# A linear-attention block with a gated FFN in split float32: four x tiles turned on VectorE through DRAM, a carried product in the down projection, and a new instruction order

## Chip, core and metric

The kernel runs on one core of one Trainium2 chip. The metric is the device time of one execution in microseconds (us). Engines: TensorE (PE, matmuls; PEld is its weight load), VectorE (DVE), ScalarE (ACT), GpSimd (POOL), SyncE (SP, which here only issues DMAs).

## The reference

S = 2048 tokens, D = 512, 32 heads of 16, F = 1792, all float32:

```python
xn = layernorm(x)
q, k, v = split(xn @ wqkv)
phi = lambda t: where(t > 0, t + 1, exp(t)) + 1e-6
pq, pk = phi(q), phi(k)
kv = einsum("bhsd,bhse->bhde", pk, v);  z = einsum("bhsd->bhd", pk)
o = einsum("bhqd,bhde->bhqe", pq, kv) / (einsum("bhqd,bhd->bhq", pq, z)[..., None] + 1e-6)
s = o @ wo
g = silu((gelu(xn @ w_gate) * (xn @ w_up)) @ w_down)
return x + s * g
```

v is never made: the kernel sums pk^T xn over the tokens (the tiles gps), multiplies it by wv and wo once, and gets a 512x512 matrix M, so that s = (pq / den) @ M.

## The kernel before

**Numbers.** A float32 matmul takes several passes of TensorE. The kernel instead writes a value as hi + lo, both in the type fp32r (the helper `split`: a cast on ACT for hi, a subtraction on DVE or POOL for lo), and does three one-pass matmuls, hi hi, hi lo and lo hi (`three`, issued by `Sum.add`, L531).

**Products.** The large products use Strassen's method in Winograd's form: seven products of half-size blocks for eight. Product 1 is copied by ACT from one bank of PSUM (X) into another (Y) as a seed, so that two results share it. This holds for k and q (`rest`, `first_products`), for gate and up (`quad`: 28 quads of seven products) and for the down projection (`down_strassen`: two passes p = 1 and 0 of NU = 7 steps u, each in two halves r, with seven products of three matmuls). Products 2, 6, 5, 7, 3, 4 go on in the banks X, Y and Z; six results of each half are added by DVE to the sums `acc` in SBUF, or copied there by ACT where u = 0 and the sum is new.

**Stages.** Stage A (to about 140 us) takes the 16 tiles of 128 tokens in eight pairs (`tokens`, NP = 8): load x, normalise (`ln`: statistics and xn on DVE, the power on POOL), transpose by PE into PSUM (`transp`: four 128x128 transposes a tile, L696, an ACT copy behind), split, multiply; q goes to DRAM (`q_d`). Pairs 0 and 1 are done with plain products, the others with Strassen's. 14 matmuls on a constant (`warm`, L561; 28 instructions, 5.82 us in the timeline) stand ahead of the first transposition. Between the stages come z (`run_z`, two split matmuls), kv and M. Then the FFN runs for the second half of the tokens (p = 1) and for the first (p = 0). Some work for later stages is done beside it: `prep_early` splits the weights of three quads and stores them in DRAM, `den` makes the denominators of a tile, `turn` loads a tile of q, divides it, transposes it by VectorE's 32x32 squares and stores it in `t_d`. The host has permuted the columns of wq so that the squares suffice.

**The end.** `attn` loads a chunk of 512 tokens of the turned q, splits it, and multiplies by M: chunk 2 behind pass 1, chunk 3 among the last down products, then chunks 0 and 1 (CHUNKS). `out_tile` loads x^T (`sxr`), multiplies the product by g, adds x^T and stores; the very last tile in two halves of columns, behind one matmul sum.

**The order.** Nothing is issued in program order. `do` records each operation with an engine and a duration; `Plan.order` lays them out with a forward pass over the engines, from latest start times; `KEPT` is a list of random alterations of these start times (a stretch of time and a seed each) that are applied one after the other. PE's order is first stated by hand in `pe_keys` and may be altered within `AHEAD` = 6 us. `forward` holds a model of the DMA queue (`RATES`, `HELD`, `BEHIND`). The engines in `ENGINES` run in exactly this order; SP is not among them before. `plan.due` makes an operation urgent from a given time on.

Of the kernel before, what the change touches and what calls it, by code (L numbers as in the profile page):

```python
# [9 lines left out]
F32 = mybir.dt.float32  # L10
# [9 lines left out]
    (85, 100, [10000006]),  # L20
    (70, 85, [10000048]),
    (-1, 12, [10000061]),
    (40, 55, [10000175]),
    (135, 200, [10000200]),
    (25, 40, [10000230]),
    (40, 55, [10000342]),
    (85, 100, [10000376]),
    (40, 55, [10000415, 10000462]),
    (500, 560, [10000471]),
    (-1, 12, [10000515]),  # L30
    (500, 560, [10000523, 10000590, 10000640]),
    (115, 135, [10000649]),
    (500, 560, [10000723]),
    (115, 135, [10000785]),
    (500, 560, [10000819, 10000833]),
    (340, 420, [10000924]),
    (115, 135, [10000994]),
    (-1, 12, [10001161, 10001223, 10001300]),
    (270, 340, [10001313, 10001357]),
    (-1, 12, [10001377]),  # L40
    (500, 560, [10001410]),
    (-1, 12, [10001492]),
    (40, 55, [10001818]),
    (-1, 12, [10001854]),
    (500, 560, [10001973]),
    (340, 420, [10002732]),
    (135, 200, [10006848]),
    (85, 100, [10010611]),
    (270, 340, [10010753]),
    (40, 55, [10010839]),  # L50
    (340, 420, [10010858]),
    (500, 560, [10010942, 10011053]),
    (40, 55, [10011765]),
    (135, 200, [10011937]),
    (-1, 12, [1010000092]),
    (340, 420, [1010000637, 1010002072]),
    (25, 40, [1010003933]),
    (500, 560, [1010016325, 1010018040]),
    (70, 85, [1010018047, 1010018667, 1010018893, 1010020523]),
    (55, 70, [1010020607]),  # L60
    (85, 100, [1010021997]),
    (100, 115, [1010030646]),
    (115, 135, [1010032131]),
    (100, 115, [1010033698]),
    (500, 560, [1010034750, 1010034866]),
    (135, 200, [1010038225]),
# [5 lines left out]
RATES = 260.0, 385.0  # L72
HELD = 1.3, 2.6
# [3 lines left out]
WARM = 14, 3  # L77
ENGINES = {mybir.EngineType.PE, mybir.EngineType.Activation, mybir.EngineType.DVE, mybir.EngineType.Pool}
# [52 lines left out]
class Plan:  # L131
# [179 lines left out]
    def forward(self, pe):  # L311
# [9 lines left out]
        while any(cands.values()):  # L321
# [43 lines left out]
            if o.eng == "SP":  # L365

                if written > o.end:
                    o.end = free["SP"] = max(o.end, dma - BEHIND)
                dma = max(dma, o.end) + o.kb / (RATES[0] if o.end < 3.0 else RATES[1])
# [26 lines left out]
def kernel(  # L396
# [78 lines left out]
    q_d = dram_view([NT, KT, P, P], "q_d", NT)  # L475
    g_d = dram_view([D, S // 2], "g_d", NT // 2)
    t_d = dram_view([KT, P, S], "t_d", NT)
    s_d = dram_view([D, NC], "s_d", KT)
# [70 lines left out]
    ones = const("ones", [P, P])  # L549
# [3 lines left out]
    ident = const("ident", [P, P])  # L553
# [9 lines left out]
    idle = bank(0, "warm", (P, P))  # L563
    do("PE", 0.427 * 10, warm, idle, ones, key="warm")
# [59 lines left out]
    CL = 2  # L624
    a21 = [[tile_in("up", 15 + 2 * lo + k, [P, D], F32R, f"a21{lo}{k}") for k in range(2)] for lo in range(2)]
# [8 lines left out]
    def ln(*ts):  # L634
        n = len(ts)
        mv = little("mv", f"mv{ts[0]}", [P, n, 2])
        for i, t in enumerate(ts):
# [7 lines left out]
           rstd, ve, neg_half)  # L645
        for i, t in enumerate(ts):
            xns[t] = U("xn", range(4, 9), f"xn{t}")
            do("DVE", 0.46, lambda o, i, m, r: nc.vector.tensor_scalar(o, i, m, r, op0=ALU.subtract, op1=ALU.mult),
               xns[t], xs.pop(t), mv[:, i, 0:1], rstd[:, i:i + 1], name=f"xn{t}")
# [38 lines left out]

    def transp(n, i):
        t = tokens[n][i]  # L690

        pt = bank(3 + 2 * n + i if 0 < 2 * n + i < 2 * CL else 1, f"pt{t}", (P, KT, P))

        def run(o, a, b):
            for k in range(KT):
                nc.tensor.transpose(o[:, k, :], a[:, k * P:(k + 1) * P], b)  # L696
            if n == 0 and i == 0:
                warm(idle(), ones(), WARM[1])
        do("PE", 0.4, run, pt, xns[t], ident, key=("T", n, i), name="T", more=(idle,) if n == 0 and i == 0 else ())
# [3 lines left out]
        xts[n, i] = v.part((v.res[i],), (slice(None), i))  # L703
        copy("ACT", xts[n, i], pt, D, f"xt{n}{i}")
        pts[n, i] = pt
# [16 lines left out]
    def split_x(n, i):  # L722
        if i == 0 and n == 0:
            for s in range(2):
                split(xrows("h", s, s + 1, [0]), xrows("l", s, s + 1, [0]), pts[0, 0][:, 2 * s:2 * s + 2], 2 * P, "Xa")
# [13 lines left out]
    def split_xn(t):  # L739
        h = U("xnh", range(9, 12), f"xnh{t}", F32R)  # L740
        lo = U("xnl", range(12, 15), f"xnl{t}", F32R)
        copy("ACT", h, xns[t], D, "xnh")
        tt("DVE", "sub", lo, xns[t], h, D, "xnl")
# [97 lines left out]
    for n in range(NP):  # L841
        if n == 0:
            ln(tokens[n][1])
        else:
            ln(*tokens[n])
        for i in range(2):
            load_next()
            transp(n, i)
            split_x(n, i)
# [42 lines left out]
    pe_keys.append(("T", 0, 0))  # L892
# [64 lines left out]
    EARLY = range(11, 14)  # L957
# [5 lines left out]

    GT = []
# [6 lines left out]
    ones_r = const("ones_r", [P, P], F32R)  # L971
    copy("ACT", ones_r, ones, P)
    zh, zl = tile_in("up", 34, [P, D], F32R, "zh"), tile_in("up", 35, [P, D], F32R, "zl")
    split(zh, zl, zacc, D, "z")
    pz = bank(7, "pz")

    def run_z(o, a, h, lo):
        nc.tensor.matmul(o, a, h, start=True, stop=False)
# [25 lines left out]
    def den(p, t):  # L1004
# [5 lines left out]
        do("DVE", 0.11, lambda o, i: nc.vector.tensor_add(o, o, i), r.map(lambda ap: ap.rearrange("p (s h) -> p s h", s=KT)),  # L1010
           den_eps.map(lambda ap: ap.unsqueeze(1).to_broadcast([P, KT, H // KT])))
        do("DVE", 0.28, lambda o: nc.vector.reciprocal(o, o), r, port=False)

    mask2 = const("mask2", [P, P])
# [113 lines left out]
    def h_sums(p, u):  # L1128
        def t():
            i = ring("hsum", range(4))  # L1130
# [6 lines left out]

    def down_strassen(p, u, first):

        for r in range(2):  # L1140
# [6 lines left out]
            def out(ps, key, new=False):  # L1147

                half, chunk = {11: (0, 0), 21: (1, 0), 12: (0, 1), 22: (1, 1)}[key]
                o = acc[p, 4 * chunk + 2 * half + r]  # L1150
                if first and new:
# [276 lines left out]
```

## Time and profile before

| | |
|---|---|
| time, median of 3 runs | 604.92 us (604.47 to 605.88) |
| the profiled execution's own time | 605.64 us |
| its span, first to last instruction | 603.5 us |
| granted TensorE clock, mean | 0.997 |
| DMA packets and bytes | 73384, 137.09 MB, mean 227 GB/s |

The span is shorter than the execution's time by what lies ahead of the first and behind the last instruction. In tables of groups a row gives line, engine, operation, output<-inputs, shapes and count, then busy time, mean ns of one, idle time just before and what ended it. Matmuls overlap, so that the mean of one is longer than the distance from one to the next. In the rows of time the first number is the start in us, the second the length.

### The profile page before, as it was taken

Reading aid. Unit: us, or ns where it says so; the run is one execution under the profiler, and the core shown is the slowest. Engines: PE = TensorE matmul, PEld = TensorE weight load, DVE = VectorE, ACT = ScalarE, POOL = GpSimd, SP = SyncE. Lnnn points to the kernel's source line nnn. Section 1 sums busy time; section 2 is a strip of 40 time slices with the busy share of each in tenths; the row PEclk is TensorE's granted clock in tenths of the full one; section 3 lists DMA queues with packets and bytes.
Section 4 is the critical chain, followed back from the end, with each engine's and each line's share of the span. In section 5 each row is a group of like instructions: output and inputs, shape, how many; then the busy total and the mean of one; then the engine's idle time right before and its main releaser. Section 6 shows DMA issues by size and latency. Waiting matters only on the chain.

```text
span 603.5 us, 7883 instructions
## 1 busy us (share of the span) xinstructions
PE 594.2 (98%) x2636; PEld 483.4 (80%) x2636; DVE 517.0 (86%) x819; ACT 347.1 (58%) x627; POOL 243.0 (40%) x237
## 2 busy tenths in 40 slices
PE   9999999999999999999999999999999999999996
PEld 7887877788878888888888777788888888886885
DVE  6999998787689899999899766668899898987995
ACT  6687888787576655655344566655353444445530
POOL 4456757757535372615053830522222130325000
PEclk9999999999999999999999999999999999999998
DMA  7259954779863344667964999744555665568577
GB/s 243 70 154 273 292 187 137 220 212 352 349 232 129 134 175 174 223 225 270 364 213 153 364 394 351 299 164 153 191 193 191 204 215 190 194 202 295 195 252 259
DMA packets 73384, 137.09 MB, mean 227 GB/s; under 512 B 4352, under 2 KB 43264, under 8 KB 69248
## 3 DMA queue, kind: packets, MB, share of 16 engines
q1 hardware_dynamic: 73344, 136.59, 64.8%
q8 instruction: 21, 0.34, 0.2%
q14 instruction: 19, 0.16, 0.1%
HBM read 85.72 MB, written 50.86 MB: 226 GB/s over the span
## 4 chain that ended last, share of the span: by engine, by line
PE 87%; DVE 6%; DMA 4%; ACT 1%; issue 1%; POOL 0%; DVEq 0%; ACTq 0%; POOLq 0%
PE FX L531 24%; PE FZ L531 12%; PE dX L531 11%; PE gps L531 7%; PE FY L531 6%; PE dZ L531 5%; PE X L531 5%; PE dY L531 3%; PE Z L531 2%; PE k L531 2%; PE q L531 2%; PE sps L531 2%; DMA sxr<-in_A_xT 2%; PE Y L531 1%; DMA pql<-t_d 1%
## 5 line engine op out<-in xcount | busy, mean ns | idle before, releaser
L531 PE MATMUL FX<-Xh,w 128*128 128x512 f32 x448 | 135.2, 391 | 0.0
L531 PEld LDWEIGHTS FX<-Xh,w 128*128 128x128 f32 x448 | 83.9, 188 | 18.3 <-ACT fu L498 0.6
L1194 POOL TENSOR_TENSOR h<-h,g 128x512 f32<-128x512 f32 x28 | 41.3, 1475 | 99.5 <-DVE h L504 95.5
L531 PE MATMUL FZ<-Xh,w 128*128 128x512 f32 x224 | 69.8, 393 | 0.0
L531 PE MATMUL FX<-Xl,w 128*128 128x512 f32 x224 | 68.9, 390 | 0.1
L1154 DVE TENSOR_TENSOR acc<-acc,dX 128x512 f32<-128x512 f32 x76 | 51.8, 681 | 19.4 <-PE dX L531 18.9
L498 ACT CAST hfh<-sums 128x512 fp32r<-128x512 f32 x56 | 34.5, 622 | 48.9 <-DVE sums L504 48.4
L498 ACT COPY fu<-FX 128x512 f32<-128x512 f32 x56 | 32.9, 587 | 42.2 <-PE FX L531 40.6
L504 POOL TENSOR_TENSOR tmp<-raw 128x256 f32<-128x256 f32 x28 | 27.4, 992 | 66.9 <-DVE w L504 35.3
L531 PEld LDWEIGHTS FZ<-Xh,w 128*128 128x128 f32 x224 | 42.0, 188 | 9.9 <-issue 1.0
L531 PEld LDWEIGHTS FX<-Xl,w 128*128 128x128 f32 x224 | 42.0, 188 | 9.2 <-ACT fu L498 0.5
L504 DVE TENSOR_TENSOR hfl<-sums,hfh 128x512 fp32r<-128x512 f32 x56 | 42.5, 764 | 4.2 <-ACT hfh L498 3.3
L531 PE MATMUL dX<-hfl,dh 128*128 128x512 f32 x112 | 43.9, 394 | 1.1 <-DVE acc L1154 0.6
L1007 POOL TENSOR_TENSOR qz<-qz,zq 128x512 f32<-128x512 f32 x16 | 23.4, 1465 | 50.9 <-DMA qz<-q_d 44.5
L531 PE MATMUL dX<-hfh,dl 128*128 128x512 f32 x112 | 43.7, 391 | 0.0
L531 PE MATMUL dX<-hfh,dh 128*128 128x512 f32 x112 | 43.7, 392 | 0.0
L504 POOL TENSOR_TENSOR sums<-draw 128x256 f32<-128x256 f32 x28 | 22.0, 795 | 45.0 <-DMA draw<-in_B_w_down 34.3
L1154 DVE TENSOR_TENSOR acc<-acc,dZ 128x512 f32<-128x512 f32 x52 | 35.5, 683 | 3.9 <-PE dZ L531 3.8
L498 ACT CAST hfh<-h 128x512 fp32r<-128x512 f32 x42 | 26.0, 621 | 15.3 <-POOL h L1194 5.4
L531 PE MATMUL FY<-Xh,w 128*128 128x512 f32 x112 | 34.3, 390 | 0.3 <-ACT FY L498 0.3
L531 PE MATMUL FZ<-Xl,w 128*128 128x512 f32 x112 | 34.3, 390 | 0.0
L504 DVE TENSOR_TENSOR hfl<-h,hfh 128x512 fp32r<-128x512 f32 x42 | 32.8, 781 | 0.0
(197 smaller groups left out, 1490.6 us busy)
## 6 DMA issues: line engine op xcount, KB each, us to landing
w<-w_d SPq DMA_DIRECT2D x17, 1792.0 KB, 7.6
w_d<-w SPq DMA_DIRECT2D x11, 1792.0 KB, 8.0
draw<-in_B_w_down SPq DMA_DIRECT2D x14, 512.0 KB, 6.1
w_d<-we SPq DMA_DIRECT2D x18, 256.0 KB, 3.3
x<-in_A_x SPq DMA_DIRECT2D x16, 256.0 KB, 4.0
q_d<-qp SPq DMA_DIRECT2D x16, 256.0 KB, 2.9
qz<-q_d SPq DMA_DIRECT2D x16, 256.0 KB, 4.5
q<-q_d SPq DMA_DIRECT2D x16, 256.0 KB, 3.3
```

Source lines behind the costliest of these rows:

```text
L498: do("ACT", act(n, src.psum), lambda o, i: nc.scalar.copy(o, i), dst, src, name=name)
L504: do(eng, c, lambda o, p, q: getattr(e, f"tensor_{op}")(o, p, q), dst, a, b, name=name)
L531: nc.tensor.matmul(o if r is None else o[:, r], a, b, start=first, stop=made == self.passes[r], skip_group_check=self.on or r is not None)
L1007: do("POOL", pool(D), lambda o, z: nc.gpsimd.tensor_mul(o, o, z.unsqueeze(1).to_broadcast([P, KT, P])), rows_of(q), zq, name="u")
L1154: do("DVE", dve(D), lambda o, i: nc.vector.tensor_add(o, o, i), o, ps, name="acc")
L1194: do("POOL", pool(NC), lambda o, i: nc.gpsimd.tensor_mul(o, o, i), h, g, name="h")
```

## The change

Without the list of alterations, which is replaced by one of 175 rows, the changes are:

- Pairs 6 and 7 (TX = 6; four tiles) are not transposed by PE. ACT makes their xn (Identity with scale and bias from two small DVE results), it is stored in DRAM and loaded in another order, and VectorE's squares turn it into SBUF (`squares`). The host permutes the columns of x for that, and the other tiles' xn is written back into the old order by a strided write.
- The first tile is transposed in two halves; fewer warming matmuls.
- `prep_early` uses one buffer for all four groups of a quad.
- z is one float32 matmul on `ones` and `zacc`.
- `den`: the small sum and the reciprocal once for four tiles. DENS goes from 6 to 8.
- `down_strassen`: the sum of product 5 over all u is kept in two tiles (`fifth`) and enters at the last u; X after product 6 is copied into Y as a second seed; the order of products on PE is stated as 1, 6, 2, 5, 7, 3, 4, before 1, 6, 5, 2, 7, 3, 4.
- Chunk 3 (SPLIT) is split in `turn` and stored as hi and lo; `attn` loads both.
- The last product is done in two halves of 256 columns; x^T of the last chunk goes into tiles that the FFN has left (FREED).
- SP joins ENGINES; the model of the DMA queue gets other numbers.

```diff
-RATES = 260.0, 385.0
-HELD = 1.3, 2.6
+RATES = 385.0, 385.0
+HOLE = 2.0, 1.3
+HELD = 1.55, 2.6
-WARM = 14, 3
-ENGINES = {mybir.EngineType.PE, mybir.EngineType.Activation, mybir.EngineType.DVE, mybir.EngineType.Pool}
+WARM = 12, 2
+ENGINES = {mybir.EngineType.PE, mybir.EngineType.Activation, mybir.EngineType.DVE, mybir.EngineType.Pool, mybir.EngineType.SP}
...
+    TX = 6
+    XDUE = 0
...
+        if ts[0] in [t for p in tokens[TX:] for t in p]:
+            nb = little("nb", f"nb{ts[0]}", [P, n])
+            do("DVE", 0.11, lambda o, i, r: nc.vector.scalar_tensor_tensor(o, i, -1.0, r, op0=ALU.mult, op1=ALU.mult),
+               nb, mv[:, :, 0], rstd)
+            for i, t in enumerate(ts):
+                xns[t] = U("xn", range(4, 9), f"xn{t}")
+                do("ACT", 0.72, lambda o, i, r, b: nc.scalar.activation(o, i, AF.Identity, bias=b, scale=r),
+                   xns[t], xs.pop(t), rstd[:, i:i + 1], nb[:, i:i + 1], name=f"xn{t}")
+                rows = xns[t].map(lambda ap: ap.rearrange("p (q e) -> p q e", e=P))
+                dma(xn_d(t, t).map(lambda ap: ap.rearrange("q s e -> s q e")), rows, 256)
+            return
...
+    def squares(dst, src):
+        do("DVE", 1.03, lambda o, i: nc.vector.transpose(
+            o.rearrange("p g (s t) -> p g t s", t=KT), i.rearrange("p (t g d) -> p g t d", t=KT, d=32)),
+           dst, src, name="turn", port=False)
...
+        if n >= TX:
+            s = U("xq", [34, 35], f"xq{t}")
+            dma(s.map(lambda ap: ap.rearrange("p (i e) -> p i e", e=P)),
+                xn_d(t, t).map(lambda ap: ap.rearrange("q (s i) e -> (q s) i e", i=KT)), 256)
+            squares(xts[n, i], s)
+            pts[n, i] = xts[n, i]
+            return
...
-            v = raw_tile(R1, f"we{q}{g}", [P, 2, D]) if g % 2 else None
-            f = [(half(v, hl) if v else tile_in("up", 34 + hl, [P, D], F32, f"we{q}{g}{hl}")).map(
+            v = raw_tile(R1, f"we{q}{g}", [P, 2, D])
+            f = [half(v, hl).map(
...
-    def run_z(o, a, h, lo):
-        nc.tensor.matmul(o, a, h, start=True, stop=False)
-        nc.tensor.matmul(o, a, lo, start=False, stop=True)
-    do("PE", 0.5, run_z, pz, ones_r, zh, zl, key="z")
+    do("PE", 0.9, lambda o, a, b: nc.tensor.matmul(o, a, b, start=True, stop=True), pz, ones, zacc, key="z")
...
             prod(X, 1, False)
             copy("ACT", Y, X, D, "seed")
+            prod(X, 6, True)
             prod(Y, 2, True)
-            out(Y, 11, True)
-            prod(X, 6, True)
-            out(X, 12, True)
-            prod(Z, 5, False)
-            out(Z, 22, True)
+            out(Y, 11)
+            if last:
+                copy("ACT", Z, fifth[p][r], D, "seed")
+            prod(Z, 5, last)
+            if last:
+                out(Z, 22)
+                out(Z, 12)
+            else:
+                out(Z, 5)
+            copy("ACT", Y, X, D, "seed")
             prod(X, 7, True)
             out(X, 22)
-            prod(Z, 3, True)
-            out(Z, 12)
+            prod(Y, 3, True)
+            out(Y, 12)
             prod(X, 4, True)
-            out(X, 21, True)
+            out(X, 21)
...
+        if t // 4 not in SPLIT:
+            dma(to[0], v, 256)
+            return
+        h = U("qz", [35], f"qh{t}", F32R).map(lambda ap: ap.rearrange("p (g c) -> p g c", c=P))
+        copy("ACT", h, v, D, "pqTh")
+        do("DVE", dve(D), lambda o, i, j: nc.vector.tensor_sub(o.bitcast(F32R), i, j), v, v, h, name="pqTl")
+        for d, s in zip(to, (h.map(lambda ap: ap.bitcast(F32)), v)):
+            dma(d, s, 256)
...
+            if (c, n) == (CHUNKS[-1], KT - 1):
+                halves = []
+                for m in range(2):
+                    cs = slice(m * NC // 2, (m + 1) * NC // 2)
+                    ps = bank(ring("sps", [3, 4, 2, 0, 1]), f"sps{c}{n}{m}", (P, NC // 2))
+                    Sum(ps).add(("S", c, n, m), *three([[v[:, k, rows] for v in M] for k in range(KT)],
+                                                       [[v[:, cs] for v in f] for f in forms_]), name="S", cost=SHORT)
+                    halves.append(ps)
+                out_tile(c, n, halves)
+                continue
...
-            xr = U("g", SPOTS, f"sxr{c}{n}")
+            xr = U(*(("xr", FREED) if c == CHUNKS[-1] else ("g", SPOTS)), f"sxr{c}{n}")
...
-    DENS = 6
+    DENS = 8
+    EORDER = (1, 6, 2, 5, 7, 3, 4)
+    SPLIT = (3,)
```

More of the change, by code (lines that the diff above doesn't have):

```diff
@@ L547, in const @@
         return small[name]
-    ones = const("ones", [P, P])
+    blk = tile_in("cpool", "blk", [P, 4, P], F32, "blk", 4)
+    ones, ident, mask2 = (blk.part(blk.res[i:i + 1], (slice(None), i)) for i in range(3))
     do("DVE", 0.2, lambda o: nc.vector.memset(o, 1.0), ones, port=False)
@@ L703, in transp, with run @@
         xts[n, i] = v.part((v.res[i],), (slice(None), i))
+        if n >= TX:
[5 more added lines that the diff above has]
+            return
+        front = n == 0 and i == 0
+        pt = tile_in("ps", 3 + 2 * n + i if 0 < 2 * n + i < 2 * CL else 1, [P, KT, P], F32, f"pt{t}", 2 if front else 1)
+        for h in range(2 if front else 1):
+            v = pt.part(pt.res[h:h + 1], (slice(None), slice(2 * h, 2 * h + 2))) if front else pt
+            def run(o, a, b, h=h):
+                for k in range(2 if front else KT):
+                    j = 2 * h + k
+                    nc.tensor.transpose(o[:, k, :], a[:, j * P:(j + 1) * P], b)
+                if front and h:
+                    warm(idle(), ones(), WARM[1])
+            do("PE", 0.25 if front else 0.5, run, v, xns[t][0], ident, key=("T", n, i, h) if front else ("T", n, i), name="T",
+               more=(idle,) if front and h else ())
         copy("ACT", xts[n, i], pt, D, f"xt{n}{i}")
@@ L1136, in h_sums @@
             h_form(u, slot, o)
+    fifth = {}
     def down_strassen(p, u, first):
+        if first:
+            fifth[p] = [spare(p).part(spare(p).res[7:8], (slice(None), 5)), tile_in("cpool", "blk", [P, D], F32, f"fifth{p}")]
+        last = u == NU - 1
         for r in range(2):
@@ L1145, in prod, with out @@
                 Sum(ps, on).add(("E", p, u, r, i), *three([[f[:, r * P:(r + 1) * P] for f in ds[u, a]]], [hforms[u, b]]), name="down")
[L1147 to L1151, printed above, removed]
+            def out(ps, key):
+                half, chunk = {11: (0, 0), 21: (1, 0), 12: (0, 1), 22: (1, 1), 5: (0, 0)}[key]
+                o = fifth[p][r] if key == 5 else acc[p, 4 * chunk + 2 * half + r]
+                if first:
                     copy("ACT", o, ps, D, "acc")
@@ L1335, in sums @@
     def sums(c):
+        if c == CHUNKS[-1]:
+            return [("S", c, n) for n in range(KT - 1)] + [("S", c, KT - 1, m) for m in range(2)]
         return [("S", c, n) for n in range(KT)]
```

327 lines of the change are left out of this document (239 added, 88 removed).

## The prediction

> **What bounds the kernel now.** I read the page's first part and chain of waits, then the table of windows, then the waits of TensorE (PE).
>
> ```profile
> span 603.5 us, 7883 instructions
> PE 594.2 (98%) x2636; PEld 483.4 (80%) x2636; DVE 517.0 (86%) x819; ACT 347.1 (58%) x627; POOL 243.0 (40%) x237
> PE 87%; DVE 6%; DMA 4%; ACT 1%; issue 1%; POOL 0%; DVEq 0%; ACTq 0%; POOLq 0%
> 230.27 2.72 PE FX L531 x12
> ```
>
> PE is busy 594.2 of 603.5 us and has 87% of the chain. Twelve 128x512 matmuls take 2.72 us, so one slot is 0.227 us (the 390 ns of the groups overlap). Little idle time is left to win in the middle:
>
> ```profile
> 80.00:140.00 60.00, 59.65 (x271) 47.99 (x270) 52.01 (x78) 47.87 (x90) 40.73 (x38) 1.00 0.63 199
> 200.00:300.00 100.00, 100.00 (x443) 82.81 (x442) 93.31 (x148) 53.53 (x98) 39.81 (x41) 1.00 0.59 213
> 540.00:560.00 20.00, 18.81 (x78) 13.60 (x77) 16.42 (x26) 11.14 (x21) 10.96 (x10) 1.00 0.74 260
> 560.00:580.00 20.00, 20.00 (x90) 16.57 (x89) 20.00 (x35) 9.09 (x15) 0.00 (x0) 1.00 0.65 229
> 594.67 3.33 PE L531 MATMUL sps<-pql,M 128*128 128x512 f32 x14
> ```
>
> The columns are stretch, length, then busy time of PE, weight loads, VectorE (DVE), ScalarE (ACT) and POOL, PE's clock, DMA share and GB/s. In the FFN (200 to 300) PE has no gap although DVE is 93% busy. PE's last matmul ends at 594.67 + 3.33 = 598.0. Its 9.3 us of idle time are thus 1.1 at the start, 5.5 behind its last matmul and 2.7 between, of which 1.19 lie in 540 to 560. So a time changes here by matmul slots added or removed, by what precedes the first product, by stalls near 550, and by the end.
>
> **Tiles turned without PE (gain 1.8).** The few words say six x tiles; the code says pairs 6 and 7 of eight, so four tiles. Each loses one group of four transposes:
>
> ```profile
> 95.28 0.60 PE L696 MATMUL pt<-ident,xn 128*128 128x128 f32 x4
> 95.63 0.71 PE L531 MATMUL X<-kq,Xh 128*128 128x512 f32 x2
> 96.18 0.63 PE L531 MATMUL X<-kq,Xl 128*128 128x512 f32 x2
> L1260 DVE STREAM_TRANSPOSE sums<-q 128x512 f32<-128x512 f32 x16 | 17.5, 1096 | 0.4
> L648 DVE TENSOR_SCALAR xn<-x,mv,rstd 128x512 f32<-128x512 f32 x16 | 10.3, 658 | 0.7 <-POOL rstd L644 0.7
> L761 ACT ACTIVATE kr<-kr 128x512 f32<-128x512 f32 x16 | 10.1, 633 | 0.4
> q_d<-qp SPq DMA_DIRECT2D x16, 256.0 KB, 2.9
> q<-q_d SPq DMA_DIRECT2D x16, 256.0 KB, 3.3
> 77.47 0.94 SPq L494 DMA_DIRECT2D x<-in_A_x  x2
> ```
>
> The group starts at 95.28 and the next at 95.63 (0.35); the pair behind it takes 0.55 instead of 0.454 (0.10). So 0.45 a tile, 4 x 0.45 = 1.8 us off PE. What comes in per tile: on ACT one activation, 0.63 (no such Identity is in the trace; bounds 0.57, the shortest copies, to 0.63 plus a table load), against the copy out of PSUM that goes; on DVE a transposition, 1.10, and a small product, less xn, 0.66: some 0.55 more, 2.2 in all, into 60 - 52.01 = 8 us of idle DVE; on SP a store and a load. The path to the turned tile is 0.63 + 2.9 + 3.3 + 1.1 = 8 us longer; the last x tiles are asked for at 77.47 and their transposes in question ran at 112 and 115, so it lies in front of need by over 20 us. I take 0 on the path; bounds 0 and one uncovered store for each pair, 2 x 2.9 = 5.8. The load waits on SP for the store to land; behind it in SP's fixed order stand weight loads and the stores of q and of early weights. Four such waits are 4 x 2.9 = 11.6 us of a queue whose engines are 0.63 busy in that stretch.
>
> The Trainium skill (VectorE: DVE Perf Modes, Rules for kernel authors) advises TensorE for a 128x128 transposition that may end in PSUM, so it speaks against this step. By that rule the term is 0 and the sum 1.8 us higher; the rows say that here PE is the scarce engine, and the 1.10 us on VectorE is larger but has room.
>
> **The z sum (loss 0.4).** Two split matmuls become one in plain f32, and four DVE and ACT steps go.
>
> ```profile
> 147.70 0.39 PE L978 MATMUL pz<-zh,ones_r 128*128 128x512 f32 x1
> 165.51 1.72 PE pm L1041 x4
> ```
>
> pm is such an f32 product, two instructions each of 1.72 / 4 = 0.43: 0.86 less two slots of 0.227 is +0.4.
>
> **The front (gain 0.5).** The warming matmuls fall from 14 to 12 and from 3 to 2 (two instructions each), and the first tile is transposed and split in halves.
>
> ```profile
> 1.12 5.82 PE L561 MATMUL warm<-ones 128*128 128x128 f32 x28 [1.12 <-DVE neg_half L552]
> 5.28 0.55 DVE L648 TENSOR_SCALAR xn<-x,mv,rstd 128x512 f32<-128x512 f32 x1 [0.67 <-POOL rstd L644]
> 6.77 0.60 PE L696 MATMUL pt<-ident,xn 128*128 128x128 f32 x4
> 8.14 1.17 PE L531 MATMUL k<-kq,Xh 128*128 128x512 f32 x4
> 9.29 1.75 POOL L504 TENSOR_TENSOR kq<-wk,kq 128x512 fp32r<-128x512 f32 x1 [1.00 <-ACT kq L498]
> 11.10 0.19 PEld L531 LDWEIGHTS k<-kq,Xh 128*128 128x128 f32 x1 [0.39 <-POOL kq L504]
> ```
>
> xn is ready at 5.83 and its transposes start at 6.77, so up to 0.9 is lost to warming; four instructions fewer of (6.77 - 1.12) / 28 = 0.20 give 0.8, the halves 0.2 to 0.3 more. But at 11.10 PE waits for a weight form made on POOL, which no edit makes earlier by itself. Bounds: nothing (that form decides) and 1.2; I take 0.5.
>
> **Down products (0).** The sum of product 5 is carried from one u to the next in two tiles, and X is copied a second time into Y. Per half (2 passes x 7 x 2 halves = 28) matmuls stay 21.
>
> ```profile
> L1154 DVE TENSOR_TENSOR acc<-acc,dX 128x512 f32<-128x512 f32 x76 | 51.8, 681 | 19.4 <-PE dX L531 18.9
> L1154 DVE TENSOR_TENSOR acc<-acc,dZ 128x512 f32<-128x512 f32 x52 | 35.5, 683 | 3.9 <-PE dZ L531 3.8
> L1154 DVE TENSOR_TENSOR acc<-acc,dY 128x512 f32<-128x512 f32 x24 | 16.3, 680 | 0.6 <-PE dY L531 0.6
> L498 ACT COPY dY<-dX 128x512 f32<-128x512 f32 x28 | 16.0, 570 | 22.4 <-DVE acc L1154 12.4 <-PE dX L531 9.1
> PE dY L531 <- ACT dY L498: 0.3, 1, 0.3
> ```
>
> Before: 76 + 52 + 24 = 152 additions. After: none at the first u, five at each of five, six at the last: 31 per pass and half, 124. DVE loses 28 x 0.68 = 19 us; ACT gains 28 second seeds, four of the carried sum and four first copies, 36 x 0.57 = 21, into its idle 42%. Both were covered by PE, so neither gives time. The new wait: product 7 must wait for the second seed, which waits for Y's addition. Between product 2 and product 7 stand product 5 (3 slots, 0.68) and at least one FFN product (6 slots, 1.36), together 2.04, against 0.68 + 0.57 = 1.25 and the hand-overs. Covered: 0. If not, the nearest row is the one stall that PE had on a seed, 0.28 us, 28 times: 7.8.
>
> **Chunk 3's forms and the last chunk (gain 0.6 and 1.6, loss 0.2).** Chunk 3 is split at its turning and loaded as two forms, the x tiles of the last chunk get tiles of their own, and its last product is done in two halves of 256 columns.
>
> ```profile
> PE dX L531 <- DVE acc L1154: 0.6, 2, 0.5
> PE sps L531 <- ACT pql L498: 0.4, 1, 0.4
> 589.72 5.97 DMA sxr<-in_A_xT
> 595.79 0.69 DVE L504 TENSOR_TENSOR acc<-acc,sxr 128x512 f32<-128x512 f32 x1 [2.65 <-DMA sxr<-in_A_xT]
> 599.05 0.74 DVE L1323 TENSOR_TENSOR acc<-acc,sps 128x256 f32<-128x256 f32 x2
> 599.72 0.75 DVE L504 TENSOR_TENSOR acc<-acc,sxr 128x256 f32<-128x256 f32 x2
> 119.15 0.30 PEld L531 LDWEIGHTS X<-kq,Xl 128*128 128x128 f32 x2 [0.78 <-DVE qp L763]
> ```
>
> Four casts and four subtractions leave the stretch in which DVE is busy 20.00 of 20, so of the 1.19 us of PE stalls at 540 to 560 I take half, 0.6 (bounds: all, 1.2, and the loss of as much, since the loads double to 2 MB where DMA already has 0.74). At the end DVE waits 2.65 us for an x tile asked for at 589.72 and is then behind: its last half ends at 599.72 + 0.75 = 600.47. With x early it can follow PE: 598.0, one half product 0.37, one half addition 0.38, 598.8. Gain 1.6; bounds 0 (the output queue holds it as before) and 1.7. The half-width product has 24 matmuls for 12. Two weight loads that start 0.30 - 0.19 = 0.11 apart fit a 256-column slot of 0.113, so about +0.2. A 256-column split matmul is not in the trace: below, 0; above, f32's rate, pm's 0.86 / 2 = 0.43 each: 24 x 0.43 - 2.72 = +7.6. Same type as the 512-column row, so I stay near 0.
>
> **At nothing.** DVE's sums and reciprocals of the denominators by fours, two of them moved to the first pass: DVE work off the path. Early weights use one buffer twelve times in place of six: 12 x (0.62 + 0.68) + the landings come near 55 us, and in the trace these stores ran from 57.2 to 124.4, so it fits with little room:
>
> ```profile
> L494 SPq DMA_DIRECT2D w_d<-we x24: 319/330/752, 57.2 to 124.4; - x24
> ```
>
> **Sum.** -1.8 + 0.4 - 0.5 + 0.2 - 1.6 - 0.6 = -3.9 on the profiled execution's 605.64 (span 603.5 and 2.14 around it): 601.7. That execution is 0.72 above the median of 604.92, so 601.0.
>
> **Rivals.** (1) More: the front gives 1.2, all 2.7 us between and 1.7 at the end: -1.8 + 0.4 - 1.2 - 2.7 - 1.7 = -7.0, 597.9. For: the forms and buffers named are those waited for. Against: a new fixed order has stalls of its own. (2) Less: front, join and end stay bound as before, -1.8 + 0.4 + 0.2 = -1.2, 603.7. For: out stores and x loads share one queue at the end. (3) Slower by the second seed: at DVE 93% busy an addition can stand behind others; each half then holds PE at product 7. Above 3.9 / 28 = 0.14 us each it eats the gain; at 0.28 the time is 608.8. Against: the first seed has the same form and stalled PE once in 28. (4) The turned tiles come late, 5.8: 606.8. Against: 20 us of lead. (5) Half-width matmuls at f32's rate: 601.0 + 7.4 = 608.4. That the change does less than it says is settled: four tiles, not six, and the sum has four.
>
> **How the numbers follow.** Forecast 50% (own range 599.3 to 602.8), more 15, less 13, seeds 11, turned tiles 6, half width 5. A measurement here can tell about 0.2%, 1.2 us. Faster: 50 + 15 + half of less, 72%; same: the other half and a little of the late tiles, 9; slower: 19. The range 597.5 to 607.0 leaves out (3), (5) and the best of (1).
>
> **What would show it.** Right: PE's rows 48 transposes in place of 64; the first k product near 7.5; PE ending near 595; DVE's last addition within 1 us of PE's end; additions 124; no PE wait on Y's seed. Wrong: PE waiting for dY's copy or a turned tile at 95 to 120, 256-column matmuls over 0.2 us apart, or a gap before the second quad for weights.

## The result, and the profile after

The changed kernel takes 602.93 us (median of 10 runs, 602.18 to 603.38) against 604.97 (603.54 to 607.25) for the kernel before in the same series: a ratio of 0.9958, 95% interval 0.9949 to 0.9968, or 2.0 us less by the medians. The time lies inside the range and on the forecast side, just above the forecast's own range (599.3 to 602.8); the gain is half of the 3.9 us that was summed up. The two profiled executions, 605.64 and 602.79 us, differ by more than the medians, 2.4 us in their spans; the account below is of these two.

The page of the changed kernel, first part:

```profile
span 601.1 us, 7826 instructions
PE 593.4 (99%) x2626; PEld 481.2 (80%) x2626; DVE 499.3 (83%) x768; ACT 367.4 (61%) x663; POOL 242.0 (40%) x237
```

DVE lost 17.7 us of work and ACT gained 20.3, all parts of the change together, near the 19 and 21 of the prediction for the down products alone. PE has ten matmul records fewer: 16 transposes and 6 warming ones less, 12 more from the two halves of the last product. The rows at the start and the end (start, length, engine, line, operation):

```profile
1.12 4.30 PE L695 MATMUL warm<-blk 128*128 128x128 f32 x24 [1.12 <-DVE neg_half L687]
5.90 0.66 PE L866 MATMUL pt<-blk,xn 128*128 128x128 f32 x4 [0.48 <-DVE xn L796]
6.39 0.61 PE L695 MATMUL warm<-blk 128*128 128x128 f32 x4
7.02 0.75 PE L665 MATMUL k<-kq,Xh 128*128 128x512 f32 x2
...
20.60 0.61 PE L665 MATMUL q<-a,Xh 128*128 128x512 f32 x2
...
585.83 11.19 PE L665 MATMUL sps<-pql,M 128*128 128x512 f32 x60
597.54 0.42 DVE L638 TENSOR_TENSOR acc<-acc,sxr 128x256 f32<-128x256 f32 x1
```

The first product starts at 7.02 (before: 8.14). PE ends at 585.83 + 11.19 = 597.02, 1.0 earlier than before (by the prediction's terms it would be 598.0 - 2.3 = 595.7), and DVE's last addition at 597.96, 0.94 behind it (before: 600.47 - 598.0 = 2.47 behind). So the span lost 1.0 on PE and 1.5 in the tail. The group of 60 holds 36 full and 24 half-width matmuls: (11.19 - 0.17 for the overlap of the last - 36 x 0.227) / 24 = 0.119 us for a half, a loss of 24 x 0.119 - 12 x 0.227 = 0.14.

What PE had less to do is 4 x 0.45 = 1.8 of transposes, 6 x 0.20 = 1.2 of warming, less 0.4 for z and 0.14 for the halves: 2.46. PE ended only 1.0 earlier, so 1.5 us of new gaps stand between its matmuls. The table of windows shows little of them, since a matmul's record is longer than its slot and covers a short gap. I therefore took, from every matmul record, the distance to the next one less the slot of its kind (2.72 / 12 = 0.2267 for a split product of 512 columns, 0.43 for plain f32, 0.1125 a transpose, 0.20 warming, 0.119 a half, 0.11 for pkv), and added them up by stretch. The warming counts as work here, at 0.20 throughout although its distance changes (see e2), so a run with 1.2 more of it shows 1.2 less in the first column. The first column also holds the 1.1 us ahead of the first matmul. Counted so, the kernel before has 9.5 us of gaps behind its first matmul, where the prediction saw 2.7 in the busy time. All kernels of the study, of one profiled execution each:

```
gaps of PE, us        0-20  20-80 80-140 140-320 320-540 540-end  all  slots
before                1.86  1.23   1.38   0.19    3.13    2.81   10.6  587.3
after                 2.55  2.61   2.24   0.42    1.98    2.27   12.1  584.8
e1_no_dram_trip       2.67  2.63   1.50   0.37    1.90    2.25   11.3  584.8
e2_old_warm           1.33  2.63   1.50   0.35    1.92    2.50   10.2  586.0
e3_last_whole         3.27  2.62   2.06   0.36    1.91    2.08   12.3  584.7
e4_sp_by_framework    3.13  2.61   3.50   0.53    1.96    2.17   13.9  584.8
e5_no_alterations     4.20  2.33   2.88   2.03    4.43    4.84   20.7  584.8
e6_all_by_pe          3.99  2.32   1.48   0.77    3.88    6.26   18.7  586.6
e7_no_split           3.70  2.32   2.87   1.98    4.94    6.45   22.3  584.8
e8_old_down           4.89  2.06   2.77   4.21    4.62    3.49   22.0  584.8
e9_stage_a_order      3.12  1.56   0.85   2.17    2.11    2.12   11.9  584.8
e10_six_pairs_drawn   2.74  1.75   1.70   0.91    3.23    4.68   15.0  584.8
e11_all_by_pe_drawn   2.93  1.33   1.13   0.13    3.70    3.04   12.3  586.6
e12_x_in_old_places   3.78  2.39   2.87   1.99    4.45    4.83   20.3  584.8
```

(e8 keeps the new slots; its down products have as many matmuls.) Before to after: stage A from 20 to 140 us got 2.24 us of new gaps, 1.38 of them before 80 us; 320 to 540 lost 1.15; the end 0.54. The same in windows, first the kernel before, then after (PE, weight loads, DVE, ACT, POOL, clock, DMA share, GB/s):

```profile
20.00:140.00 120.00, 119.41 (x544) 96.03 (x543) 109.13 (x172) 93.47 (x171) 75.83 (x71) 1.00 0.67 202
320.00:400.00 80.00, 79.17 (x341) 62.84 (x340) 58.94 (x90) 45.70 (x76) 33.15 (x29) 1.00 0.81 306
```

```profile
20.00:140.00 120.00, 119.12 (x526) 94.13 (x525) 107.38 (x170) 93.02 (x169) 76.81 (x71) 1.00 0.70 212
80.00:140.00 60.00, 59.94 (x261) 47.11 (x260) 52.25 (x76) 48.49 (x89) 39.96 (x37) 1.00 0.69 217
320.00:400.00 80.00, 79.66 (x346) 64.02 (x345) 54.49 (x79) 53.00 (x88) 32.19 (x29) 1.00 0.83 312
```

From 320 to 400 PE did 5 matmuls more in the same time, with DVE 4.5 us less busy and ACT 7.3 more. From 20 to 140 it did 18 matmuls less, 16 of which are the transposes: next to nothing of the freed time was used for other products.

### The profile page after: what moved, and what is told of

Same layout as the page of the kernel before. It is cut to its first block, busy times and chain, and to the rows that moved or that the text cites. A ratio compares the mean times of both kernels' runs of the same rounds, so it can differ in the third digit from the quotient of the medians.

```text
span 601.1 us, 7826 instructions
## 1 busy us (share of the span) xinstructions
PE 593.4 (99%) x2626; PEld 481.2 (80%) x2626; DVE 499.3 (83%) x768; ACT 367.4 (61%) x663; POOL 242.0 (40%) x237
## 4 chain that ended last, share of the span: by engine, by line
PE 85%; DVE 6%; DMA 6%; issue 1%; ACT 1%; SPq 0%; ACTq 0%; DVEq 0%
PE FX L665 25%; PE FZ L665 13%; PE dX L665 12%; PE FY L665 6%; PE gps L665 6%; PE dY L665 6%; PE X L665 4%; PE dZ L665 3%; DMA g<-g_d 2%; PE Z L665 2%; PE q L665 2%; PE sps L665 2%; PE k L665 2%; DMA pqh<-t_d 1%; PE Y L665 1%
## 5 line engine op out<-in xcount | busy, mean ns | idle before, releaser
L1374 POOL TENSOR_TENSOR h<-h,g 128x512 f32<-128x512 f32 x28 | 38.9, 1390 | 150.5 <-DVE h L638 150.2
L665 PE MATMUL FZ<-Xh,w 128*128 128x512 f32 x224 | 68.3, 391 | 0.0
L632 ACT COPY dY<-dX 128x512 f32<-128x512 f32 x56 | 32.0, 571 | 40.0 <-DVE acc L1328 30.6
L638 POOL TENSOR_TENSOR tmp<-raw 128x256 f32<-128x256 f32 x28 | 24.6, 886 | 47.2 <-ACT fu L632 24.1
L1328 DVE TENSOR_TENSOR acc<-acc,dX 128x512 f32<-128x512 f32 x48 | 32.9, 685 | 11.3 <-PE dX L665 10.7
L638 DVE TENSOR_TENSOR hfl<-sums,hfh 128x512 fp32r<-128x512 f32 x56 | 39.9, 721 | 2.5 <-ACT hfh L632 1.7
L1328 DVE TENSOR_TENSOR acc<-acc,dY 128x512 f32<-128x512 f32 x48 | 32.8, 684 | 10.8 <-PE dY L665 10.6
L638 POOL TENSOR_TENSOR sums<-draw 128x256 f32<-128x256 f32 x28 | 23.5, 850 | 34.9 <-DMA draw<-in_B_w_down 26.1
L638 DVE TENSOR_TENSOR hfl<-h,hfh 128x512 fp32r<-128x512 f32 x42 | 34.1, 817 | 1.6 <-ACT hfh L632 1.6
L638 DVE TENSOR_TENSOR h<-fu,FZ 128x512 f32<-128x512 f32 x28 | 19.2, 687 | 18.4 <-ACT fu L632 13.3
```

Of the source, the lines that this page charges most:

```text
L632: do("ACT", act(n, src.psum), lambda o, i: nc.scalar.copy(o, i), dst, src, name=name)
L638: do(eng, c, lambda o, p, q: getattr(e, f"tensor_{op}")(o, p, q), dst, a, b, name=name)
L665: nc.tensor.matmul(o if r is None else o[:, r], a, b, start=first, stop=made == self.passes[r], skip_group_check=self.on or r is not None)
L1328: do("DVE", dve(D), lambda o, i: nc.vector.tensor_add(o, o, i), o, ps, name="acc")
L1374: do("POOL", pool(NC), lambda o, i: nc.gpsimd.tensor_mul(o, o, i), h, g, name="h")
```

## The experiments

In e1 to e4 the order of the changed kernel is written out as a list of operations, so that an edit can't draw another order. In e5 to e8 and e12 the list of alterations is empty, for kernels that differ in one part but have had no order searched for them. e9 to e11 have orders of their own, found by equal means where they are compared.

### e1: without the trip through DRAM

```diff
-dma(xn_d(t, t)..., rows, 256)
-dma(s..., xn_d(t, t)..., 256)
-squares(xts[n, i], s)
+squares(xts[n, i], xns[t])
```

> The changed kernel with its order of instructions written out as a list and held, and the four turned tiles' store to DRAM and load back left out: VectorE turns the wrong rows of xn, so q and k of these tokens are wrong. Theory order (the slots that the four tiles free are eaten by gaps that the new order has in stage A, wherever the tiles come from): PE reaches the end of stage A within 0.3 us of the changed kernel, 602.9 us give or take 0.4. Theory load (the turned tiles or their transfers come late): the gaps behind 80 us shrink by 0.9 or more, 602.0 or less.

602.8 us, ratio 0.9966 (0.9953 to 0.998), against 0.9958 for the changed kernel: no gain. In the gaps 80 to 140 fell from 2.24 to 1.50, which alone would look like a price of the trip, but e2, which makes the trip, has 1.50 too. The runs show no cost of the trip above that scatter; it is hidden, as predicted.

### e2: the old warming

```diff
-WARM = 12, 2
+WARM = 14, 3
```

> The changed kernel in its held order, with 14 and 3 warming matmuls as before. Theory warm (the front's gain of about half a microsecond comes from the shorter warming): the first transposes start at 6.7 in place of 5.9 and PE stays 0.4 to 0.8 behind, 603.3 to 603.7 us. Rival (the load of wk decides, as the chain of the changed kernel's front shows): the first transposes are later but at 20 us PE is less than 0.2 behind, 602.9 to 603.1.

602.1 us, ratio 0.9955 (0.9943 to 0.9967): the same as with less warming within the intervals, and below what both the theory and the rival expected. Its timeline of PE:

```profile
1.11 4.72 PE L652 MATMUL warm<-blk 128*128 128x128 f32 x28 [1.11 <-DVE neg_half L644]
6.06 0.66 PE L823 MATMUL pt<-blk,xn 128*128 128x128 f32 x4 [0.22 <-DVE xn L753]
6.55 0.83 PE L652 MATMUL warm<-blk 128*128 128x128 f32 x6
7.17 0.73 PE L622 MATMUL k<-kq,Xh 128*128 128x512 f32 x2
...
20.58 0.61 PE L622 MATMUL q<-a,Xh 128*128 128x512 f32 x2
```

The longer warming costs 0.15 at the first product, and the first q product starts at 20.58 against 20.60. What the warming gave up became a gap: 1.33 + 1.2 = 2.53 in the first column, against 2.55. The front is thus set by when operands are there, not by PE's warming: from 5 to 20 us the weight loads of the changed kernel wait 0.9 for xn, 0.7 and 0.4 for forms of x (Xl, b) and 0.2 for a form of a weight (kq).

Even with the old warming PE waits 0.22 for xn, and its 28 matmuls take 4.72 us, where the same 28 took 5.82 before. Matmul by matmul, the warming ones start 0.213 us apart at first and 0.112 later. The step comes at 6.2 us in the profile of before, at 4.0 here, and between 4.0 and about 6.7 in the 14 profiles; the granted clock of these rows is 1.00 all the time. PE from 4.0 to 5.4 us, before and in e2 (9 and 15 matmuls):

```profile
4.00:5.40 1.40, 1.40 (x9) 1.00 0.89 297
4.00:5.40 1.40, 1.40 (x15) 1.00 0.97 291
```

So the bound that the prediction read off the old rows (0.9 lost to warming) was one of that execution, and the four matmuls that it took off were of the closer kind, 4 x 0.112 = 0.45 and not 0.8.

### e3: the last product as one sum of 512 columns

```diff
-for m in range(2):
-    cs = slice(m * NC // 2, (m + 1) * NC // 2)
-    Sum(ps).add(("S", c, n, m), *three(..., [[v[:, cs] for v in f] for f in forms_]), cost=SHORT)
+Sum(ps).add(("S", c, n, 0), *three(..., forms_))
```

> The changed kernel in its held order, its last product done in one sum of 512 columns (the second half's matmuls are empty). Theory: VectorE's last addition is 0.4 to 0.6 later behind PE's end, PE's end 0.1 earlier, 603.2 to 603.5 us. Rival (the output queue holds the end, so the halves bring nothing): 602.8 to 603.0.

603.65 us, ratio 0.9976 (0.9966 to 0.9987), 0.7 us above the changed kernel by medians. The end of its timeline:

```profile
586.07 11.04 PE L622 MATMUL sps<-pql,M 128*128 128x512 f32 x48
598.40 0.42 DVE L595 TENSOR_TENSOR acc<-acc,sxr 128x256 f32<-128x256 f32 x1
```

PE ends at 597.11 and DVE at 598.82, 1.71 behind instead of 0.94. So 0.77 of the 1.53 that the tail gained is the halving; the other half is there without it. In e3 DVE waits 1.31 us for PE ahead of the last product's additions and for no x tile, while before it waited 2.65 for one.

### e4: SP's order left to the framework

```diff
-ENGINES = {..., mybir.EngineType.Pool, mybir.EngineType.SP}
+ENGINES = {..., mybir.EngineType.Pool}
```

> The changed kernel in its held order on the four compute engines, with SP taken out of the engines whose order is kept, so that the framework orders the DMAs. Theory (the transfers have slack, SP's order is worth little): within 0.4 us of 602.9. Rival (the kept order is what lets the rest arrive in time): new waits of PE on what a DMA brings, 604 or more.

604.26 us, ratio 0.9993 (0.9981 to 1.0006): 1.3 us above the changed kernel by medians, and no longer told apart from the kernel before. Waits of PE from 80 to 140 us, where the changed kernel has none over 0.2:

```profile
PE X L622 <- DVE qp L891: 0.9, 1, 0.9
```

What qp waited for leads back to the queue: ACT's cast of an early weight, a DVE step on that weight behind it, then in DVE's fixed order qp. The rows of e4, SP's first:

```profile
77.76 1.06 SPq L585 DMA_DIRECT2D x<-in_A_x  x2
78.91 0.88 SPq L585 DMA_DIRECT2D w_d<-we  x2
84.55 0.62 ACT L589 CAST we<-tmp 128x512 fp32r<-128x512 f32 x1 [1.13 <-DMA w_d<-we]
85.20 0.69 DVE L595 TENSOR_TENSOR we<-tmp,we 128x512 fp32r<-128x512 f32 x1 [0.98 <-ACT we L589]
```

The changed kernel issues these two stores ahead of the x tiles:

```profile
78.10 0.81 SPq L628 DMA_DIRECT2D w_d<-we  x2
80.60 0.96 SPq L628 DMA_DIRECT2D x<-in_A_x  x2
```

There the second store has landed at 81.69, in e4 at 84.45, and until then the one buffer of the early weights can't be written again. "It fits with little room", which the prediction put at nothing, thus holds only with this order of the DMAs.

The gaps of that stretch are 3.50 (after 2.24, e2 1.50). The order of the DMA issues, which the prediction carried at no price of its own, holds more than half of the whole gain. How much of the 1.3 us goes through this one wait is not shown.

### e5: no alterations

```diff
-KEPT = [ ... 175 rows ... ]
+KEPT = []
```

> The changed kernel with an empty list of alterations, so that its order is the planner's first one; the base of the next three runs, in which one part each is undone and the order is laid out anew in the same way. Theory order: the alterations took gaps out of every stage, so 606 to 611 us, with PE's gaps larger in the front, in stage A, at 320 to 400 and at 540 to 580. Rival (the alterations fit the model and not the chip): within 1.5 us of 602.9.

610.94 us, ratio 1.0102 (1.0079 to 1.0126): the altered start times are worth 8.0 us, four times what the change gave in all, and spread over every stage (20.7 us of gaps instead of 12.1). The kernel is the base of e6 to e8 and e12.

### e6: all tiles turned by PE, no alterations

```diff
-    TX = 6
+    TX = 8
```

> As e5, with TX = 8: PE transposes all sixteen tiles. Theory slots (each turned tile frees 0.45 us of PE and its path is hidden): 1.3 to 2.3 us slower than e5. Theory load (the turned tiles' work and transfers cost stage A what they free): within 0.7 us of e5 or faster, with PE's gaps at 80 to 140 smaller by 1 us or more.

609.49 us, ratio 1.0076 (1.0049 to 1.0104): 1.4 us less than e5 by medians (the intervals overlap), although PE has 1.8 us more to do. From 80 to 140 us, where the turned tiles are made and used, its gaps are 1.48 against 2.88: of the 1.8 that the turned tiles free, 1.4 comes back as gaps, and 0.4 is left. The 2.88 holds over three profiles: e7 and e12, whose order is e5's up to this point, have 2.87 there; the 1.48 is one profile. Ahead of 80 us e5 and e6 have the same order, so their difference of 0.2 there is scatter. At the end nothing of the 0.4 is left, and e6 is the faster; its order is another one from 86 us on.

### e7: chunk 3 not split at its turning, no alterations

```diff
-    SPLIT = (3,)
+    SPLIT = ()
```

> As e5, with SPLIT empty: chunk 3 is loaded as one and split beside the last down products, as before the change. Theory (the casts and subtractions held PE near 550): 0.6 to 2 us slower than e5, all of it at 540 to 580. Rival (the wait for the two loads takes the place of the wait for the forms): within 0.4 us.

612.95 us, ratio 1.0142 (1.0111 to 1.0174): 2.0 above e5. Behind 580 us PE waits 1.5 for an addition of the down products, where e5 has no wait over 0.2. The rows of DVE show what stood ahead of that addition:

```profile
580.77 0.69 DVE L1357 TENSOR_TENSOR g<-g,sps 128x512 f32<-128x512 f32 x1 [0.71 <-DMA g<-g_d]
...
582.98 0.69 DVE L1357 TENSOR_TENSOR g<-g,sps 128x512 f32<-128x512 f32 x1 [0.93 <-DMA g<-g_d]
583.59 0.68 DVE L1152 TENSOR_TENSOR acc<-acc,dX 128x512 f32<-128x512 f32 x1
```

Two products with g wait for g's load, and the addition waits behind them in DVE's fixed order. So most of the 2.0 is one late addition, held up by a load and not by DVE's work on the forms, which the theory meant; its size came out, not its mechanism. Whether the early split always spares that addition is open.

### e8: the old down products, no alterations

```diff
-    EORDER = (1, 6, 2, 5, 7, 3, 4)
+    EORDER = (1, 6, 5, 2, 7, 3, 4)
...
-            prod(Z, 5, last)
...
-            copy("ACT", Y, X, D, "seed")
+            prod(Z, 5, False)
+            out(Z, 22, True)
```

> As e5, with the down products of the kernel before (no carried sum of product 5, one seed, six results added, the order 1, 6, 5, 2, 7, 3, 4). Theory (VectorE's additions and ScalarE's seeds were both covered): within 0.6 us of e5, PE's gaps at 200 to 540 the same within 0.5. Rival (VectorE's 19 us less work removes gaps of PE): 1 us or more slower than e5, with new gaps in the FFN.

612.76 us, ratio 1.0132 (1.0109 to 1.0156): 1.8 above e5. The stretch 140 to 320 in e5 and then in e8:

```profile
140.00:320.00 180.00, 179.00 (x795) 146.21 (x794) 156.75 (x232) 111.05 (x207) 84.66 (x85) 1.00 0.65 236
```

```profile
140.00:320.00 180.00, 178.35 (x784) 144.16 (x785) 157.85 (x240) 104.19 (x194) 84.18 (x83) 1.00 0.64 232
```

PE does 11 matmuls less there, and the gaps are 4.21 instead of 2.03; 1.35 of that is given back behind 540. So without alterations the rival holds: undoing the carried product costs about 2 us. But DVE's additions are only part of the way: the weight loads of PE that wait in this stretch of e8 wait for additions (acc) 0.8 us in all (e5: 0.6), for ACT's copies of FFN products (fu, FY) 1.3 (e5: none over 0.2) and for forms made by DVE (hfl, dl) 2.7 (e5: 1.6). The two orders differ from 13 us on, so part of it may be the luck of an order. Where the order has been fitted to the old products it costs nothing here: before, this stretch has 0.19.

### e9: the changed kernel with another order for stage A

```diff
-        for lo, hi, draws in KEPT:
-            for n in draws:
-                best = self.altered(n, lo, hi, pe, *best)
-        return [o for _, o in best[1]]
+        return [by[n] for n in ORDER_OF_AFTER]
```

(The name of the list is that of e1 to e4; the list is the new one.)

> The changed kernel, its computation untouched, with more random alterations drawn for stage A alone (12 to 140 us) and kept where the planner's own end came earlier; the resulting order is written out. Theory order (the gaps of stage A are of the order): the gaps between 20 and 140 us, 4.8 us in the changed kernel, fall by 1 or more, 601.0 to 602.0 us. Theory load: they stay within 0.5 of 4.8, 602.5 to 603.3.

601.76 us (601.52 to 603.05), ratio 0.9949 (0.9936 to 0.9963), the lowest of the study, though its interval overlaps that of the changed kernel. Stage A, 20 to 140, and the waits of PE at 200 to 260:

```profile
20.00:140.00 120.00, 119.52 (x536) 96.58 (x536) 107.08 (x174) 94.36 (x170) 74.99 (x72) 1.00 0.71 213
```

```profile
PE dX L622 <- ACT dY L589: 1.2, 1, 1.2
```

With the same computation 10 more matmuls fit into stage A than in the changed kernel; its gaps are 2.41 instead of 4.85. The first 20 us and a wait for a seed at the second stretch give 0.57 + 1.75 of that back. So the new gaps of stage A are not a price that the turned tiles force: an order without them exists. From 20 to 140 us it has 2.41 where before has 2.61, so up to there it keeps the whole 1.8, give or take the scatter of a profile. No kernel with all tiles on PE had this search on stage A, so it is not a comparison of the two ways.

### e10 and e11: six pairs, and all eight, by PE, each with an order searched equally long

```diff
-        for lo, hi, draws in KEPT: ...
+        return [by[n] for n in ORDER_OF_AFTER]
```

e11 has TX = 8 and its own list besides.

> As e5 (turned tiles, no alterations of the list), then altered by a search of fixed length; to be compared with the next run, which had a search of the same length with all sixteen tiles transposed by PE. Theory slots: 1.3 us or more faster than the next run. Theory load: not faster than it by more than 0.5.

> As e6 (all tiles by PE), altered by a search of the same length as e10. Theory slots: 1.3 us or more slower than e10. Theory load: within 0.5 of e10 or faster, with smaller gaps at 80 to 140.

605.78 (ratio 1.0011, 1.0002 to 1.002) for six pairs, 604.21 (0.9991, 0.9982 to 1.0) for eight: all tiles on PE is 1.6 faster, which is the side of "theory load". Up to 140 us the gaps are 6.19 and 5.39, so of the 1.8 freed the turned tiles keep 1.0 there. That is lost again later, 0.8 from 140 to 320 and 1.6 behind 540 (with 0.5 regained between), where no x tile is turned any more. This pair therefore shows no gain from turning, but its sign at the end may be the luck of two orders.

### e12: x tiles of the last chunk in the old places, no alterations

```diff
-            xr = U(*(("xr", FREED) if c == CHUNKS[-1] else ("g", SPOTS)), f"sxr{c}{n}")
+            xr = U("g", SPOTS, f"sxr{c}{n}")
```

> As e5, with the x tiles of the last chunk in the ring of places that they had before the change. Theory (they came late for want of a place): VectorE waits for one and its last addition falls 2 us or more behind PE's end, 0.9 in e5; 612.0 to 612.8 us. Rival (the queue of stores holds the loads, wherever they go): within 0.5 of e5's 610.9.

611.3 us, ratio 1.0105 (1.0088 to 1.0121), as e5. DVE ends 0.99 us behind PE (e5: 0.92). Its waits behind 575 us have a row that e5 doesn't have:

```profile
DVE acc L462 <- DMA sxr<-in_A_xT: 2.1, 3, 1.2
```

So the x tiles do come late from the old places, as the theory said, and the new places take these waits away. But the last of the three ends at 600.86 us, and by PE's end at 605.26 DVE has caught up: in this order the waits cost nothing.

## Why the prediction was right in sign and twice too large

**Turned tiles, -1.8: the step that failed.** The prediction put: "So 0.45 a tile, 4 x 0.45 = 1.8 us off PE", and "some 0.55 more, 2.2 in all, into 60 - 52.01 = 8 us of idle DVE". The slots did go, by the groups of the changed kernel:

```profile
L866 PE MATMUL pt<-blk,xn 128*128 128x128 f32 x48 | 7.5, 278 | 0.9 <-DVE xn L796 0.7
```

Its DMA issues (count, size, us to landing) and, by tile, the two operations that came in (shortest, middle and longest in ns, first and last start):

```profile
xn_d<-xn SPq DMA_DIRECT2D x4, 256.0 KB, 2.6
xq<-xn_d SPq DMA_DIRECT2D x4, 256.0 KB, 3.3
```

```profile
L788 ACT ACTIVATE xn<-x,nb,rstd x4: 802/815/819, 89.3 to 106.3; 128x512 f32<-128x512 f32 x4
L840 DVE STREAM_TRANSPOSE xt<-xq x4: 1082/1100/1112, 99.2 to 116.3; 128x512 f32<-128x512 f32 x4
```

The durations are as estimated but for ACT's 0.81 (0.63 was taken), and DVE is 52.25 busy from 80 to 140 against 52.01. The path was hidden (e1). What failed is the step from a freed slot to a gain: the prediction took 1.8 us less work on PE for 1.8 us less time. A slot without a transpose is filled only if the next product's forms are there earlier. Two pairs of kernels whose orders were made alike put the gain at the end of stage A at 0.4 (e5, e6) and, give or take the scatter of a profile, 1.0 (e10, e11) of 1.8, and neither shows any at the end of the kernel. In the changed kernel itself 2.24 us of new gaps ate it; 1.38 of them lie ahead of 80 us, before any turned tile is made, and e9 has only 0.33 there: that part is the order's. The share of the rest is open, since two profiled executions (after and e2), whose orders differ in the warming alone, differ by 0.7 from 80 to 140. That PE's feeders DVE and ACT are busy 107.38 and 93.02 of 120 us in stage A may be why an order that uses the slots is hard to find; it does not forbid one, since e9 has 107.08 and 94.36. By the rule of the Trainium skill (VectorE: DVE Perf Modes, Rules for kernel authors) that the prediction weighed, the term is 0; at the end of the kernel the two pairs side with it, though no run shows a reason in DVE's speed.

**The front, -0.5.** PE's place at 20 us is 1.2 - 0.69 = 0.5 ahead of before, the size that was put. But e1 and e3, whose first 20 us have the same order, are 1.2 - 0.81 = 0.4 ahead and 1.2 - 1.41 = 0.2 behind, and of before there is one profile: the agreement may be luck. Right is that the warming's 0.8 would not be had (e2). Which of the forms, the halves or the order gives the rest was not tried apart.

**z, +0.4 and halves, +0.2.** The halves took 0.14, so the rival of f32's rate is out. The timeline of PE at z:

```profile
147.62 1.02 PE L1149 MATMUL pz<-zacc,blk 128*128 128x512 f32 x2
148.07 1.03 PE L665 MATMUL FX<-Xh,w 128*128 128x512 f32 x2
148.95 0.40 PE L665 MATMUL FX<-Xl,w 128*128 128x512 f32 x1
```

From 147.62 to 148.95 are 1.33 us for z and two split products; less 2 x 0.227 that is 0.88 for z, against 0.45 before: +0.4, as predicted.

**Down products, 0.** The count of 124 was exact (48 + 48 + 10 + 10 + 8), by the groups of the changed kernel:

```profile
L1328 DVE TENSOR_TENSOR acc<-acc,dX 128x512 f32<-128x512 f32 x48 | 32.9, 685 | 11.3 <-PE dX L665 10.7
L1328 DVE TENSOR_TENSOR acc<-acc,dY 128x512 f32<-128x512 f32 x48 | 32.8, 684 | 10.8 <-PE dY L665 10.6
L1328 DVE TENSOR_TENSOR fifth<-fifth,dZ 128x512 f32<-128x512 f32 x10 | 6.8, 684 | 3.4 <-PE dZ L665 3.2
L1328 DVE TENSOR_TENSOR sums<-sums,dZ 128x512 f32<-128x512 f32 x10 | 6.8, 682 | 0.6 <-PE dZ L665 0.4
L1328 DVE TENSOR_TENSOR acc<-acc,dZ 128x512 f32<-128x512 f32 x8 | 5.3, 682 | 1.2 <-PE dZ L665 1.2
```

PE's only waits of 0.3 or more from 140 to 580 are one on a load and one on a seed:

```profile
PE sps L665 <- DMA pql<-tl_d: 0.7, 1, 0.7
PE dX L665 <- ACT dY L632: 0.3, 1, 0.3
```

That seed, at 336 us, is a first one. The second seed is seen only from start to start: it held PE up twice in 28, for 0.2 us at 221 and for 0.3 at 550, each time behind Y's addition as rival (3) said, and far from its 0.28 on every half. The later one:

```profile
549.81 0.57 ACT L632 COPY dY<-dX 128x512 f32<-128x512 f32 x1 [0.55 <-DVE acc L1328]
550.44 0.50 PE L665 MATMUL dY<-hfh,dl 128*128 128x512 f32 x1
```

"Covered by PE, so neither gives time" held from 140 to 320 (0.19 and 0.42 of gaps) but not behind: 1.15 us less from 320 to 540, a gain that the prediction did not have. That the carried product gives it is not shown: e8, without it, has only 0.19 more there than e5, and the largest single difference is a wait of before for a form of h (hfl) at 391 us, 0.7 from start to start, that the changed kernel doesn't have.

**Chunk 3, -0.6, and the tail, -1.6.** Right in size: 0.54 and 1.53. From 540 to 560 us PE's waits of before are gone, 0.5 for an addition, 0.4 for ACT's form and 0.3 for a seed; in their place PE waits 0.7 for the load of the low form, the price of doubled loads that stood among the bounds. That the split does it is not shown for this order; in e7 its worth came another way. Half of the tail is the halving (e3). The other half comes with the end of DVE's wait for x tiles, which the prediction named: the changed kernel has none behind 575 us, before 3.4 us. That new places end such waits e12 shows; whether they or the new order did it here was not tried.

The sum as measured, to the end of DVE: -1.8 + 2.24 (stage A) + 0.4 - 0.5 - 0.92 (140 to 540) - 0.54 + 0.14 - 1.53 = -2.5. The span fell by 2.4. Five terms of seven came near their sizes, one of them (the front) within the scatter of a profile; one gain was missed and one was eaten. That the missed 0.92 makes up for part of the eaten 2.24 is luck. By SP's order (e4) and the alterations (e5) the result hangs on the order as much as on any edit.

## What to carry to other kernels

Work taken off the busiest engine is a gain only where the next operand is early; price freed slots at nothing until a kernel pair with orders made alike shows otherwise. Where instruction orders are searched for, compare two computations both with the search switched off and with searches of equal length: the order's worth (8 us here) is several times that of an edit. Count gaps from start to start, not by busy time, which hides any gap that is shorter than the overlap of two records (here 0.39 - 0.227 = 0.16 us). Where a buffer is reused, ask what the queue puts ahead of the store that frees it (e4).

## What was not expected of the hardware

The order in which SP issues DMAs is worth 1.3 us with everything else held. The wait shows up on PE as one for qp, an operand made on DVE; ACT's cast and DVE's fixed order stand between it and the store that came late.

The first matmuls of an execution stand 0.213 us apart and later ones of the same kind 0.112, at a granted clock of 1.00 in the rows; the step lies between 4.0 and about 6.7 us in 14 profiles (e2).

Two profiled executions whose orders differ in the warming alone differ by 0.7 us in the gaps of a 60 us stretch (after and e2, 80 to 140), and three executions whose first 20 us are ordered alike (after, e1, e3) by 0.7 there, while the times of the ten runs spread over 1.2. One profile can't price a stall below that.

In e6 the granted clock fell in one window, with PE nearly full:

```profile
560.00:580.00 20.00, 19.70 (x71) 14.61 (x72) 16.39 (x24) 10.61 (x18) 2.20 (x2) 0.83 0.93 326
```

That profiled execution took 611.25 us, the other three of e6 609.32 to 609.60; its column from 540 us to the end in the table of gaps is too long by that.

A matmul of 256 columns took 0.119 us, just over half of the 0.227 of one with 512, although each needs its own weight load.
